# Chunk totals from a float32 exp row by POOL transfers, half of the score masks on ScalarE and GpSimd, and late first outputs, in a gated linear attention and squared-ReLU MLP kernel

## The chip, the cores and the metric

The kernel runs on one core of a Trainium2 chip. The metric is the device time in microseconds (us) of one launch. The engines are TensorE (PE, with PEld for its weight loads), VectorE (DVE), ScalarE (ACT), GpSimd (POOL) and SyncE (SP, which here issues loads and stores).

## The reference

For 4 batches and 8 heads, 768 time steps of a gated recurrence on a 48 x 48 state, then an MLP over all 3072 tokens:

```python
for t in range(S):                                   # S = 768
    state = alpha[:, :, t, :, None] * state + einsum('bhd,bhe->bhde', k[:, :, t], v[:, :, t])
    y[:, :, t] = einsum('bhd,bhde->bhe', q[:, :, t], state)
x = y.transpose(0, 2, 1, 3).reshape(B * S, H * D)    # 3072 x 384
h = x @ w_in                                         # 384 -> 2048
r = maximum(h, 0.0)
out = (r * r) @ w_out                                # 2048 -> 384
```

All inputs and the output are float32; the kernel's matmuls run in bfloat16.

## The kernel before, in words

The 3072 tokens are 24 chunks (tiles) of 128 tokens, six for each batch. Chunks 0 to 3 are done as two sets of two chunks with a layout of their own (`add_set`), chunks 4 to 23 one by one (`add_chunk`).

One chunk goes through these steps. ACT takes the logarithm of alpha into `L_s` (L600). PE multiplies it by a triangular matrix (`e_p0`, L610), which gives running sums down the chunk in a PSUM bank, and with four more matmuls of one column against a vector of ones (L612) the sum over the whole chunk, laid out with the state's rows on the partitions. ACT writes exp of the running sums as `A` (L619) and of their negatives as `Ainv` (L623), both bfloat16, and exp of the totals into `ae_s` by two small activations (L626, L629). DVE multiplies q by `A` into `qA_s` (L638) and k by `Ainv` into `kI_s` (L641). PE transposes both, DVE copies them to `qkT`. PE forms the scores in two banks a chunk (`add_scores`); from chunk 8 on two chunks' scores are one step that needs four banks. DVE multiplies each half of the scores by the triangular mask (`e_sm`, L675, 512 columns, twice a chunk). PE adds k times v onto the state (`e_ps`), DVE scales the state by the totals in `ae_s` (`e_stm`, L696), ACT casts it to `sb` (L701); the next chunk's state step and its output matmuls (`e_p3a`) need `sb`. PE forms the outputs (`e_p3a`, `e_p3b`), ACT casts them to `xn`, PE transposes them, and DVE copies them to `xT_big` (`e_xT`), which the MLP reads. POOL casts v to `vb` (L605) and the MLP's weights (L330).

The MLP works on groups of tiles, `GN = [4, 1, 1, 2, 2, ...]`. `add_moe1` is the first matmul, with a relu on ACT (L798) and a square on DVE (L811) into `gT`. The second is `add_moe2`, or, for groups 3 to 10, `add_moe2_pair`, which computes two tiles with seven half-size products in place of eight. That needs sums of blocks of `gT` (S1 to S4): S1 and S2 are DVE additions into buffers of the pool `stage` (L928), S3 and S4 are, where the group is in `BY_DMA`, accumulating transfers issued by POOL (L936). Outputs go out through SP (L853, L855, L1021).

The order of every engine's instructions is written out when the kernel is built. A planner (`Plan`) holds each step as an `Op` with an assumed duration, its dependencies, a priority (lower is earlier) and the banks that it takes, and picks step by step what can start first; the steps are then emitted in order of their planned starts, and each engine runs its own in that order. A chunk's `e_p0` may not be planned before `s <= LEAD + progress`, where progress counts the MoE work planned so far in tiles of 5.12 us. `OUT_LATE0` and `OUT_LATE` delay the store of an output by so many planned microseconds (group 0: 16, others: 3.5). `DMA_FROM`, `BUSY` and `XT_ACT` choose from which group the accumulating transfers are used and from which chunk some copies go to ACT. PE runs filler matmuls only ahead of the first second-layer matmul.

Times in the diff, such as 0.6 or 3.6, are the planner's assumptions.

Of the kernel before, what the change touches and what calls it, by code (L numbers as in the profile page):

```python
# [8 lines left out]
FP32 = mybir.dt.float32  # L9
# [55 lines left out]
class Plan:  # L65


    def __init__(self):
        self.pending = {}
        self.order = []  # L70
        self.free = {}
        self.pool = []
        self.outs = []

    def add(self, op):
        op.durs = op.eng if isinstance(op.eng, dict) else {op.eng: op.dur}
        for e in op.durs:
            self.pending.setdefault(e, []).append(op)
        return op

    def ready(self, op):
        t = op.at
        slack = PE_SLACK if "PE" in op.durs else 0.0
        if slack and self.free.get("PE", 0.0) > PE_CALM:
            slack = 0.25
        for d, x in op.deps:
            if d.done is None:
                return None
            if x is None:
                t = max(t, d.done + (slack if d.eng != "PE" else 0.0))  # L90
            else:
                t = max(t, d.start + d.dur + x)
        if op.takes is not None:
            free = [(sl.free_at(), i) for i, sl in enumerate(op.takes)]
            free = sorted((f, i) for f, i in free if f is not None)[:op.n_slots]
            if len(free) < op.n_slots:
                return None
            op.slots = [op.takes[i] for _, i in free]
            op.slot = op.slots[0]
            t = max(t, free[-1][0])  # L100
        return t
# [59 lines left out]
def kernel(  # L161
# [10 lines left out]
    nc = tc.nc  # L172
# [77 lines left out]
    NBUF = 4  # L250
    DMA_FROM = 0
    BY_DMA = {g: ("S3", "S4") if g >= DMA_FROM else () for g in range(40)}
    BUSY = 99
    CP_N = 99
    XT_ACT = 0
    L_s = big.tile([P, NBUF, H, DP], BF16)
# [4 lines left out]
    nc.vector.memset(kI_s[:, :, :, D:], 0.0)  # L261
    ae_s = big.tile([P, NBUF, NP, 2], FP32)
    nc.vector.memset(ae_s, 0.0)
# [9 lines left out]
    def pin(ins):  # L273
        tc.keep_in_program_order(ins)
# [96 lines left out]
    def add_set(u):  # L371
# [24 lines left out]
        def add_decay(a):  # L396
# [14 lines left out]
            def e_exp(out, nm, scale):  # L411
                out[a] = work.tile([P, 2, HH, D], BF16, name=nm)
                pin(nc.scalar.activation(out[a], pm[a][:, 0:HD].rearrange("p (j h d) -> p j h d", j=2, h=HH), AF.Exp, scale=scale))
# [19 lines left out]
        def e_ae(h):  # L433
            r = slice(64 * h, 64 * h + 64)
            pin(nc.scalar.activation(ae[r, :, :, h].rearrange("q c p -> q p c"),
                                     pm[0][r, HD:HD + 2 * NP].rearrange("q (p c) -> q p c", c=2), AF.Exp))
# [63 lines left out]
        def add_state(c):  # L500
# [18 lines left out]
            def e_stm():  # L519
                st4 = e["st"].rearrange("p n (j e) -> p n j e", j=2)  # L520
                pin(nc.vector.tensor_mul(st4, st4, bcast(ae[:, c], D)))
            stm = add("DVE", 0.47, e_stm, ps, ae1, **gs)
# [6 lines left out]
        def add_out(c):  # L529
# [28 lines left out]
            def e_xn():  # L558
                e["xn"] = work.tile([P, HD], BF16, name="xn")
                cast2(xn, e["xn"], e["py"][:, 0:HD])  # L560
# [21 lines left out]
    def add_chunk(s):  # L582
# [25 lines left out]
        def e_p0():  # L608
            pm = d["pm"] = psum(p0, [P, 512], FP32)
            mm(pm[:, 0:HD], lhsT=utri_b[:, 0, :], rhs=L[:, :, 0:D], start=True, stop=True)  # L610
            for p in range(NP):
                mm(pm[:, HD + p:HD + p + 1], lhsT=L[:, 2 * p:2 * p + 2, :], rhs=ones_col,  # L612
                   start=True, stop=True)
        p0 = Op("PE", 0.27, e_p0, [ln], takes=GLA_BANKS, lat=0.05, **g)
        p0.gla = s

        def e_A():
            d["A"] = work.tile([P, H, D], BF16, name="A")
            pin(nc.scalar.activation(d["A"], d["pm"][:, 0:HD].rearrange("p (h d) -> p h d", h=H), AF.Exp))  # L619

        def e_Ai():
            d["Ai"] = work.tile([P, H, D], BF16, name="Ainv")
# [10 lines left out]
        ae0 = add("ACT", 0.18, e_ae0, p0, after(ai), **g)  # L633
        ae1 = add("ACT", 0.19, e_ae1, p0, after(ae0), **g)
        p0.gives = ae1

        def e_qA():
            pin(nc.vector.tensor_mul(qA[:, :, 0:D], d["qt"], d["A"]))  # L638

# [30 lines left out]
        p2, first = d["p2"]  # L670

        def e_sm(hh):
            if hh == 0:
                d["sm"] = work.tile([P, 2, NP, P], BF16, name="sm")
            pin(nc.vector.tensor_mul(d["sm"][:, hh], d["sc"][hh], utri_b.to_broadcast([P, NP, P])))  # L675
        done = after(p2, -0.15) if first else p2
        sm0 = add("DVE", 0.6, lambda: e_sm(0), done, **g)
        sm1 = add("DVE", 0.6, lambda: e_sm(1), done, after(sm0), **g)
        p2.gives += [sm0, sm1]

        if not last:
# [8 lines left out]
            if c == 0 and s:  # L690
                prev = C[s - 2]["sb"]
            ps = plan.add(Op("PE", 0.17, e_ps, [mk, vb, ae1, prev], lat=0.16, **g))

            def e_stm():
                st4 = d["st"].rearrange("p n (j e) -> p n j e", j=2)
                pin(nc.vector.tensor_mul(st4, st4, bcast(ae, D)))  # L696
            stm = add("DVE", 0.47, e_stm, ps, ae1, prio=-2.0)

# [20 lines left out]
        if c > 0:  # L719
            p3a = plan.add(Op("PE", 0.17, e_p3a, [cp, C[s - 1]["sb"], after(sm0)], takes=GLA_BANKS, **g))  # L720
        p3b = plan.add(Op("PE", 0.25, e_p3b, [after(sm1, 0.02), sm0, vb, after(p3a)], takes=None if c else GLA_BANKS, lat=0.15, **g))

        def e_xn():
            d["xn"] = work.tile([P, HD], BF16, name="xn")
            cast(xn, d["xn"], d["py"][:, 0:HD])
# [15 lines left out]
    def add_scores(ss):  # L741
# [24 lines left out]
    OUT_LATE = 3.5  # L766
    OUT_LATE0 = 16
    RELU_PRIO = -20.0
# [6 lines left out]
    def add_moe1(g, f0, before, lo=0, hi=None, per=1):  # L775
# [27 lines left out]
        def e_sq():  # L803
# [7 lines left out]
            pin(nc.vector.tensor_mul(dst, r, r))  # L811
        fr = sq[(g - NGT, "free")] if g >= NGT else None
        o = add("DVE", 0.06 + w / 1850.0, e_sq, rl, fr, prio=SQ_PRIO)
        o.shared = True
# [5 lines left out]
    def add_moe2(g, tt, before, box, quarters, pools):  # L820

        for qd in quarters:
# [17 lines left out]
        def e_ev():  # L840
            box["ob"] = opool.tile([P, d_model], FP32, name="ob")
# [7 lines left out]
        def e_out():  # L849
# [191 lines left out]
    for g in range(NG):  # L1041
# [9 lines left out]
        if g == 0:  # L1051
            boxes = [dict() for _ in range(GN[0])]
            for part in FIRST_PARTS:
                for tt in range(GN[0]):
                    b2 = add_moe2(0, tt, b2, boxes[tt], part, FIRST)
        else:
            pools = M2_LAST if g >= NG - 2 else M2_BANKS
            if g in PAIR_SUMS or (g in (1, 2) and JOIN):
# [6 lines left out]
                if g == 2:  # L1065
                    sq[(1, "free")] = b2
# [70 lines left out]
```

## Time and profile before

| | |
|---|---|
| time, median of 3 runs | 184.35 us (184.28 to 184.57) |
| the profiled execution | 184.13 us, of which 182.4 us are its span |
| TensorE clock granted | 1.000 |
| PE busy | 175.6 us (96%) |
| DVE busy | 150.3 us (82%) |
| ACT busy | 122.4 us (67%) |
| POOL busy | 41.7 us (23%) |
| HBM | 25.17 MB read, 4.72 MB written |

The span runs from the first to the last instruction; the rest of the time lies around it. Busy times are unions of the instructions' intervals on an engine. A group's line gives line, engine, operation, output<-inputs, shapes, count | busy us, mean ns of one | idle time before it, and what ended that. A matmul's interval includes its way through the pipeline, so matmuls that follow each other overlap.

### The profile page before, as it was taken

To read this page: it belongs to the slowest core of one execution; us is meant where nothing else is said; L and a number is where in the kernel's file an instruction comes from. 1 tells how busy PE (TensorE), PEld (TensorE's weight loads), DVE (VectorE), ACT (ScalarE), POOL (GpSimd) and SP (SyncE) were. 2 spreads that over 40 slices of the span, in tenths; PEclk is the share of its full clock that TensorE was granted. 3 is DMA by queue.
4 is the path that set the end of the run, shared out by engine and by line. 5 is a ranking of instruction groups with operands and counts; after the bars stand their busy time and mean duration, and the time that the engine had idled before them with its cause. 6 is when DMAs were issued, how large, how long until landed. Compare 5 with 4: busy or idle time off the path is not lost.

```text
span 182.4 us, 5636 instructions
## 1 busy us (share of the span) xinstructions
PE 175.6 (96%) x2248; PEld 147.9 (81%) x2248; DVE 150.3 (82%) x330; ACT 122.4 (67%) x295; POOL 41.7 (23%) x59
## 2 busy tenths in 40 slices
PE   7998999999999999999999999999999999999992
PEld 2676788667776887899899899899898899899871
DVE  6599869749989699999998999899998997865310
ACT  3576579436868688976867779666778777657321
POOL 4013575251111101504024002125005004030000
PEclk9999999999999999999999999999999999999999
DMA  5999998899999779999999989999999705316113
GB/s 143 264 264 340 380 351 165 278 232 172 195 194 168 155 185 202 193 198 186 229 191 205 242 190 178 215 225 212 252 174 204 184 4 101 104 33 128 43 55 117
DMA packets 101529, 34.43 MB, mean 189 GB/s; under 512 B 92416, under 2 KB 98304, under 8 KB 101504
## 3 DMA queue, kind: packets, MB, share of 16 engines
q1 hardware_dynamic: 99200, 29.89, 75.2%
q0 software_dynamic: 2304, 4.20, 13.2%
q8 instruction: 17, 0.28, 0.7%
q14 instruction: 8, 0.07, 0.1%
HBM read 25.17 MB, written 4.72 MB: 164 GB/s over the span
## 4 chain that ended last, share of the span: by engine, by line
PE 68%; DVE 16%; SPq 5%; DMA 4%; ACT 2%; issue 2%; POOL 0%; ACTq 0%
PE bank L277 61%; PE bank L280 6%; SPq L366 5%; DVE sm L675 4%; DMA wi<-in_moe_w_in_dram 4%; DVE gT L811 2%; DVE foldT L896 2%; DVE qkT L595 2%; PE st L277 1%; DVE kI_s L641 1%; DVE sums L928 1%; DVE st L696 1%; ACT r L798 1%; DVE xT_big L595 1%; DVE ob L985 1%
## 5 line engine op out<-in xcount | busy, mean ns | idle before, releaser
L277 PE MATMUL bank<-xT_big,w_in_b 128*128 128x256 bf16 (+1 forms) x624 | 76.1, 264 | 0.9 <-POOL w_in_b L330 0.7
L798 ACT ACTIVATE r<-bank 128x512 bf16<-128x512 f32 x96 | 56.8, 600 | 18.3 <-PE bank L277 14.8
L277 PEld LDWEIGHTS <-w_in_b 128*128 128x128 bf16 x624 | 53.4, 98 | 6.8 <-POOL w_in_b L330 0.8
L811 DVE TENSOR_TENSOR gT<-r 128x512 bf16<-128x512 bf16 x96 | 42.8, 469 | 8.7 <-ACT r L798 8.4
L277 PE MATMUL bank<-w_out_b,gT 128*128 128x192 bf16 (+1 forms) x320 | 44.1, 278 | 0.1
L277 PEld LDWEIGHTS <-gT 128*128 128x128 bf16 x448 | 37.9, 98 | 6.8 <-DMA gT<-sums 0.3
L605 POOL CAST vb<-vt_s 128x384 bf16<-128x384 f32 x20 | 13.4, 691 | 53.1 <-DMA vt_s<-in_v_dram 48.6
L675 DVE TENSOR_TENSOR sm<-bank,utri_b 128x512 bf16<-128x512 f32 x40 | 24.9, 681 | 0.5 <-PE bank L277 0.5
L936 POOL DMA_DIRECT2D gT<-gT x8 | 6.9, 861 | 42.9 <-DVE sums L928 34.2
L595 DVE COPY qkT<-bank 128x1024 bf16<-128x1024 bf16 x20 | 13.7, 683 | 1.1 <-PE bank L280 1.0
L638 DVE TENSOR_TENSOR qA_s<-qt_s,A 128x384 bf16<-128x384 f32 x20 | 12.4, 620 | 2.1 <-ACT A L619 1.9
L619 ACT ACTIVATE A<-bank 128x384 bf16<-128x384 f32 x20 | 9.9, 496 | 5.5 <-PE bank L277 5.5
L277 PE MATMUL bank<-foldT,sums 128*128 128x192 bf16 x128 | 13.2, 246 | 0.0
L277 PE MATMUL bank<-foldT,gT 128*128 128x192 bf16 x128 | 13.2, 246 | 0.0
L277 PEld LDWEIGHTS <-qkT 64*128 64x128 bf16 (+1 forms) x228 | 9.1, 95 | 3.6 <-issue 1.9
L641 DVE TENSOR_TENSOR kI_s<-kt_s,Ainv 128x384 bf16<-128x384 f32 x20 | 11.9, 595 | 0.0
L600 ACT ACTIVATE L_s<-at_s 128x384 bf16<-128x384 f32 x20 | 10.5, 524 | 1.0 <-DMA at_s<-in_alpha_dram 0.7
L277 PEld LDWEIGHTS <-sums 128*128 128x128 bf16 x128 | 10.7, 98 | 0.4
L701 ACT CAST sb<-st 128x384 bf16<-128x384 f32 x16 | 7.6, 476 | 4.9 <-DVE st L696 4.8
L593 ACT CAST xn<-bank 128x384 bf16<-128x384 f32 x20 | 9.7, 484 | 1.8 <-PE bank L277 1.6
L277 PE MATMUL bank<-vb,sm 128*128 128x48 bf16 (+1 forms) x224 | 10.2, 183 | 0.1
L280 PE MATMUL bank<-ident_bf,qA_s 128*128 128x128 bf16 x96 | 9.3, 220 | 0.6 <-DVE qA_s L419 0.4
(93 smaller groups left out, 234.9 us busy)
## 6 DMA issues: line engine op xcount, KB each, us to landing
at_s<-in_alpha_dram SPq DMA_DIRECT2D x22, 192.0 KB, 5.0
qt_s<-in_q_dram SPq DMA_DIRECT2D x22, 192.0 KB, 4.9
kt_s<-in_k_dram SPq DMA_DIRECT2D x22, 192.0 KB, 4.5
vt_s<-in_v_dram SPq DMA_DIRECT2D x20, 192.0 KB, 4.8
out_dram<-ob SPq DMA_DIRECT2D x20, 192.0 KB, 3.5
wo<-in_moe_w_out_dram SPq DMA_DIRECT2D x4, 768.0 KB, 6.7
wi<-in_moe_w_in_dram SPq DMA_DIRECT2D x3, 768.0 KB, 7.8
gT<-gT POOLq DMA_DIRECT2D x8, 256.0 KB, 4.8
```

The costliest lines, as they stand in the source:

```text
L277: pin(nc.tensor.matmul(*a, **kw))
L280: pin(nc.tensor.transpose(*a))
L593: pin(nc.scalar.copy(out_t, in_t))
L595: pin(nc.vector.tensor_copy(out_t, in_t))
L600: pin(nc.scalar.activation(L[:, :, 0:D], d["at"], AF.Ln))
L605: pin(nc.gpsimd.tensor_copy(d["vb"], d["vt"]))
L619: pin(nc.scalar.activation(d["A"], d["pm"][:, 0:HD].rearrange("p (h d) -> p h d", h=H), AF.Exp))
L638: pin(nc.vector.tensor_mul(qA[:, :, 0:D], d["qt"], d["A"]))
L641: pin(nc.vector.tensor_mul(kI[:, :, 0:D], d["kt"], d["Ai"]))
L675: pin(nc.vector.tensor_mul(d["sm"][:, hh], d["sc"][hh], utri_b.to_broadcast([P, NP, P])))
L798: pin(nc.scalar.activation(box["r"][:, 0:w], box["ph"][:, 0:w], AF.Relu))
L811: pin(nc.vector.tensor_mul(dst, r, r))
```

## The change

What is changed, in the order of the diff:

- `Plan.held` and `wide`: a step of lower priority may not take a bank that the four-bank scores step could use, while that step waits for nothing but banks.
- `DMA_FROM = 6`: S3 and S4 of groups 3, 4 and 5 are DVE additions; groups 6 to 10 keep the accumulating transfers.
- `BUSY = 8`, `XT_ACT = 1`: from chunk 8 on the copy into `xT_big` is on ACT.
- The totals of chunks 4 to 23: the four one-column matmuls and the two small exps are gone. `A` is written in float32, with its inner order changed, so that its last row (partition 127) holds each half of the totals as one run; two transfers issued by POOL bring that row to `ae_s`, whose layout is changed to fit. `A` of the sets is float32 too; the sets keep their matmuls for the totals.
- From chunk 8 on the second half of the scores is copied by ACT, unmasked, to SBUF, and GpSimd zeroes what the mask would (`affine_select`). The first half stays a product on DVE.
- `A`, `Ainv` and `xn` have three buffers instead of four.
- Outputs: group 0's four tiles are kept in one buffer of `stage` and stored 32 planned microseconds after they are ready; groups 1 and 2 (chunks 4 and 5) 12 after; the others 3.5 as before. The sums of the pairs wait for the pair three back, instead of four, to be done with its buffer.
- `S_PRIO = -12`: sums go ahead of the chunks' steps on DVE. `LEAD = 5`.
- Second-layer matmuls of group 0 wait for the squares of their own two tiles only.

The diff, cut to that:

```diff
+    def held(self, op):
+        for w in self.wide:
+            if w is not op and w.start is None and w.prio < op.prio and all(d.done is not None for d, _ in w.deps):
+                return w.takes
+        return ()
...
-            free = [(sl.free_at(), i) for i, sl in enumerate(op.takes)]
+            held = self.held(op)
+            free = [(sl.free_at(), i) for i, sl in enumerate(op.takes) if sl not in held]
...
-    DMA_FROM = 0
+    DMA_FROM = 6
-    BUSY = 99
+    BUSY = 8
-    XT_ACT = 0
+    XT_ACT = 1
...
-    ae_s = big.tile([P, NBUF, NP, 2], FP32)
+    ae_s = big.tile([P, NBUF, 2, NP], FP32)
...
+    SEL_FROM, SEL_T, SEL_N = 8, 0.6, 1
+    RESERVE = 1
+    ROW_POOL, ROW_LAT, ROW_DMA = 0.95, 3.6, 0.15
...
-            for p in range(NP):
-                mm(pm[:, HD + p:HD + p + 1], lhsT=L[:, 2 * p:2 * p + 2, :], rhs=ones_col,
-                   start=True, stop=True)
-        p0 = Op("PE", 0.27, e_p0, [ln], takes=GLA_BANKS, lat=0.05, **g)
+        p0 = Op("PE", 0.165, e_p0, [ln], takes=GLA_BANKS, lat=0.10, **g)
...
-            d["A"] = work.tile([P, H, D], BF16, name="A")
-            pin(nc.scalar.activation(d["A"], d["pm"][:, 0:HD].rearrange("p (h d) -> p h d", h=H), AF.Exp))
+            d["A32"] = work.tile([P, 2, D, NP], FP32, name="A", bufs=3)
+            d["A"] = d["A32"].rearrange("q j d p -> q p j d")
+            pin(nc.scalar.activation(d["A"], d["pm"][:, 0:HD].rearrange("q (p j d) -> q p j d", p=NP, j=2), AF.Exp))
...
-        def e_ae0():
-            pin(nc.scalar.activation(ae[0:64, :, 0], d["pm"][0:64, HD:HD + NP], AF.Exp))
-
-        def e_ae1():
-            pin(nc.scalar.activation(ae[64:128, :, 1], d["pm"][64:128, HD:HD + NP], AF.Exp))
+        def e_ae(h):
+            pin(nc.gpsimd.dma_start(out=ae[64 * h:64 * h + D, h, :], in_=d["A32"][P - 1:P, h]))
...
+        aes = [add("POOL", ROW_POOL, lambda h=h: e_ae(h), a_, old, lat=ROW_LAT, **g) for h in range(2)]
...
+        def e_sc():
+            pin(nc.scalar.copy(sm_half(1), d["sc"][1]))
+
+        def e_sel():
+            pin(nc.gpsimd.affine_select(out=sm_half(1), in_=sm_half(1), compare_op=ALU.is_ge, fill=0.0,
+                                        base=0, pattern=[[0, NP], [1, P]], channel_multiplier=-1))
...
+        if s >= SEL_FROM and s % SEL_N == 0:
+            sm0 = add("DVE", 0.6, lambda: e_sm(0), done, **g)
+            sc1 = add("ACT", 0.485, e_sc, done, **g)
+            sm1 = add("POOL", SEL_T, e_sel, sc1, prio=-20.0)
+            p2.gives += [sm0, sc1]
...
-            ps = plan.add(Op("PE", 0.17, e_ps, [mk, vb, ae1, prev], lat=0.16, **g))
+            ps = plan.add(Op("PE", 0.17, e_ps, [mk, vb, prev], lat=0.16, **g))
...
-            stm = add("DVE", 0.47, e_stm, ps, ae1, prio=-2.0)
+            stm = add("DVE", 0.47, e_stm, ps, *aes, prio=-2.0)
...
-    OUT_LATE0 = 16
+    OUT_LATE0 = 32
+    OUT_LATE1 = 12
+    KEEP0 = 1
...
-            deps = [o for f in fs for o in sq[(g, f)]] + ...
+            deps = [o for f in fs for o in sq_of(g, tt, f)] + ...
...
+            if g == 0 and KEEP0:
+                if "ob" not in state:
+                    state["ob"] = stage.tile([P, GN[0], d_model], FP32, name="ob0", tag="stage")
+                box["ob"] = state["ob"][:, tt]
...
-        add("OUT", 0.65, e_out, ev, at=0.0).late = OUT_LATE if g else OUT_LATE0
+        add("OUT", 0.65, e_out, ev, at=0.0).late = OUT_LATE if g > 2 else OUT_LATE1 if g else OUT_LATE0
...
-        used = pairs_done[-4] if len(pairs_done) > 3 else []
+        used = pairs_done[-3] if len(pairs_done) > 2 else []
...
-    S_PRIO = -1
+    S_PRIO = -12
...
-    LEAD = 4
+    LEAD = 5
```

More of the change, by code (lines that the diff above doesn't have):

```diff
@@ L73, in __init__ @@
         self.outs = []
+        self.wide = []
     def add(self, op):
@@ L288 @@
     PAIRED = 7
+    SEL_FROM, SEL_T, SEL_N = 8, 0.6, 1
+    RESERVE = 1
+    ROW_POOL, ROW_LAT, ROW_DMA = 0.95, 3.6, 0.15
     JOIN = 0
+    PAIRS0 = 0
+    ORDERED = 1
+    PAIR0_BANKS = FIRST0 = sl_bank[4:0:-1]
+    ORDER0 = ["i", "i", "i", "i", "i", "o", "o", 4, "o", "o", 5]
     SET_BANKS = [sl_bank[0:4] + sl_bank[5:7], sl_bank[0:3] + sl_bank[5:7]]
@@ L411, in e_exp @@
             def e_exp(out, nm, scale):
-                out[a] = work.tile([P, 2, HH, D], BF16, name=nm)
+                out[a] = work.tile([P, 2, HH, D], FP32 if nm == "A" else BF16, name=nm, bufs=3)
                 pin(nc.scalar.activation(out[a], pm[a][:, 0:HD].rearrange("p (j h d) -> p j h d", j=2, h=HH), AF.Exp, scale=scale))
@@ L434, in e_ae @@
             r = slice(64 * h, 64 * h + 64)
-            pin(nc.scalar.activation(ae[r, :, :, h].rearrange("q c p -> q p c"),
+            pin(nc.scalar.activation(ae[r, :, h, :].rearrange("q c p -> q p c"),
                                      pm[0][r, HD:HD + 2 * NP].rearrange("q (p c) -> q p c", c=2), AF.Exp))
@@ L520, in e_stm @@
                 st4 = e["st"].rearrange("p n (j e) -> p n j e", j=2)
-                pin(nc.vector.tensor_mul(st4, st4, bcast(ae[:, c], D)))
+                pin(nc.vector.tensor_mul(st4, st4, bcast(ae[:, c].rearrange("q j p -> q p j"), D)))
             stm = add("DVE", 0.47, e_stm, ps, ae1, **gs)
@@ L558, in e_xn @@
             def e_xn():
-                e["xn"] = work.tile([P, HD], BF16, name="xn")
+                e["xn"] = work.tile([P, HD], BF16, name="xn", bufs=3)
                 cast2(xn, e["xn"], e["py"][:, 0:HD])
@@ L610, in e_p0 @@
             mm(pm[:, 0:HD], lhsT=utri_b[:, 0, :], rhs=L[:, :, 0:D], start=True, stop=True)
-            for p in range(NP):
-                mm(pm[:, HD + p:HD + p + 1], lhsT=L[:, 2 * p:2 * p + 2, :], rhs=ones_col,
-                   start=True, stop=True)
-        p0 = Op("PE", 0.27, e_p0, [ln], takes=GLA_BANKS, lat=0.05, **g)
+        p0 = Op("PE", 0.165, e_p0, [ln], takes=GLA_BANKS, lat=0.10, **g)
         p0.gla = s
         def e_A():
-            d["A"] = work.tile([P, H, D], BF16, name="A")
-            pin(nc.scalar.activation(d["A"], d["pm"][:, 0:HD].rearrange("p (h d) -> p h d", h=H), AF.Exp))
+            d["A32"] = work.tile([P, 2, D, NP], FP32, name="A", bufs=3)
+            d["A"] = d["A32"].rearrange("q j d p -> q p j d")
+            pin(nc.scalar.activation(d["A"], d["pm"][:, 0:HD].rearrange("q (p j d) -> q p j d", p=NP, j=2), AF.Exp))
         def e_Ai():
-            d["Ai"] = work.tile([P, H, D], BF16, name="Ainv")
+            d["Ai"] = work.tile([P, H, D], BF16, name="Ainv", bufs=3)
             pin(nc.scalar.activation(d["Ai"], d["pm"][:, 0:HD].rearrange("p (h d) -> p h d", h=H), AF.Exp, scale=-1.0))
-        def e_ae0():
-            pin(nc.scalar.activation(ae[0:64, :, 0], d["pm"][0:64, HD:HD + NP], AF.Exp))
-        def e_ae1():
-            pin(nc.scalar.activation(ae[64:128, :, 1], d["pm"][64:128, HD:HD + NP], AF.Exp))
+        def e_ae(h):
+            pin(nc.gpsimd.dma_start(out=ae[64 * h:64 * h + D, h, :], in_=d["A32"][P - 1:P, h]))
         plan.add(p0)
@@ L632, in add_chunk @@
         ai = add("ACT", 0.38, e_Ai, p0, after(a_), **g)
-        ae0 = add("ACT", 0.18, e_ae0, p0, after(ai), **g)
-        ae1 = add("ACT", 0.19, e_ae1, p0, after(ae0), **g)
-        p0.gives = ae1
+        p0.gives = ai
+        aes = [add("POOL", ROW_POOL, lambda h=h: e_ae(h), a_, old, lat=ROW_LAT, **g) for h in range(2)]
+        for x in aes:
+            x.quiet, x.moves = True, ROW_DMA
         def e_qA():
-            pin(nc.vector.tensor_mul(qA[:, :, 0:D], d["qt"], d["A"]))
+            pin(nc.vector.tensor_mul(qA[:, :, 0:D].rearrange("q (p j) d -> q p j d", j=2),
+                                     d["qt"].rearrange("q (p j) d -> q p j d", j=2), d["A"]))
         def e_kI():
@@ L670, in add_chunk, with sm_half @@
         p2, first = d["p2"]
+        def sm_half(hh):
+            if "sm" not in d:
+                d["sm"] = work.tile([P, 2, NP, P], BF16, name="sm")
+            return d["sm"][:, hh]
         def e_sm(hh):
-            if hh == 0:
-                d["sm"] = work.tile([P, 2, NP, P], BF16, name="sm")
-            pin(nc.vector.tensor_mul(d["sm"][:, hh], d["sc"][hh], utri_b.to_broadcast([P, NP, P])))
-        done = after(p2, -0.15) if first else p2
-        sm0 = add("DVE", 0.6, lambda: e_sm(0), done, **g)
-        sm1 = add("DVE", 0.6, lambda: e_sm(1), done, after(sm0), **g)
-        p2.gives += [sm0, sm1]
+            pin(nc.vector.tensor_mul(sm_half(hh), d["sc"][hh], utri_b.to_broadcast([P, NP, P])))
+        def e_sc():
[3 more added lines that the diff above has]
+                                        base=0, pattern=[[0, NP], [1, P]], channel_multiplier=-1))
+        done = after(p2, -0.15) if first else p2
+        if s >= SEL_FROM and s % SEL_N == 0:
[3 more added lines that the diff above has]
+            p2.gives += [sm0, sc1]
+        else:
+            sm0 = add("DVE", 0.6, lambda: e_sm(0), done, **g)
+            sm1 = add("DVE", 0.6, lambda: e_sm(1), done, after(sm0), **g)
+            p2.gives += [sm0, sm1]
         if not last:
@@ L691, in add_chunk @@
                 prev = C[s - 2]["sb"]
-            ps = plan.add(Op("PE", 0.17, e_ps, [mk, vb, ae1, prev], lat=0.16, **g))
+            ps = plan.add(Op("PE", 0.17, e_ps, [mk, vb, prev], lat=0.16, **g))
             def e_stm():
                 st4 = d["st"].rearrange("p n (j e) -> p n j e", j=2)
-                pin(nc.vector.tensor_mul(st4, st4, bcast(ae, D)))
-            stm = add("DVE", 0.47, e_stm, ps, ae1, prio=-2.0)
+                pin(nc.vector.tensor_mul(st4, st4, bcast(ae.rearrange("q j p -> q p j"), D)))
+            stm = add("DVE", 0.47, e_stm, ps, *aes, prio=-2.0)
             def e_sb():
@@ L720, in add_chunk @@
             p3a = plan.add(Op("PE", 0.17, e_p3a, [cp, C[s - 1]["sb"], after(sm0)], takes=GLA_BANKS, **g))
-        p3b = plan.add(Op("PE", 0.25, e_p3b, [after(sm1, 0.02), sm0, vb, after(p3a)], takes=None if c else GLA_BANKS, lat=0.15, **g))
+        p3b = plan.add(Op("PE", 0.25, e_p3b, [after(sm1, 0.02 if sm1.eng == "DVE" else 0.15), sm0, vb, after(p3a)], takes=None if c else GLA_BANKS, lat=0.15, **g))
         def e_xn():
-            d["xn"] = work.tile([P, HD], BF16, name="xn")
+            d["xn"] = work.tile([P, HD], BF16, name="xn", bufs=3)
             cast(xn, d["xn"], d["py"][:, 0:HD])
@@ L753, in add_scores @@
         plan.add(p2)
+        if len(ss) > 1 and RESERVE:
+            plan.wide.append(p2)
         for s in ss:
@@ L811, in e_sq @@
             pin(nc.vector.tensor_mul(dst, r, r))
-        fr = sq[(g - NGT, "free")] if g >= NGT else None
-        o = add("DVE", 0.06 + w / 1850.0, e_sq, rl, fr, prio=SQ_PRIO)
+        fr = sq[(g - NGT, "free")] if g >= NGT else []
+        o = add("DVE", 0.06 + w / 1850.0, e_sq, rl, *fr, prio=SQ_PRIO)
         o.shared = True
@@ L829, in add_moe2 @@
             fs = range(qd * FT // NQ, (qd + 1) * FT // NQ) if g == 0 else range(FT)
-            deps = [o for f in fs for o in sq[(g, f)]] + [w_dep("o", fs[-1] if g == 0 else FT - 1)] + ([after(before)] if before else [])
+            deps = [o for f in fs for o in sq_of(g, tt, f)] + [w_dep("o", fs[-1] if g == 0 else FT - 1)] + ([after(before)] if before else [])
             op = plan.add(Op("PE", 0.65, e_mm, deps, takes=pools if qd == 0 else None, prio=0.1 + 0.01 * g))
@@ L840, in e_ev @@
         def e_ev():
-            box["ob"] = opool.tile([P, d_model], FP32, name="ob")
+            if g == 0 and KEEP0:
+                if "ob" not in state:
+                    state["ob"] = stage.tile([P, GN[0], d_model], FP32, name="ob0", tag="stage")
+                box["ob"] = state["ob"][:, tt]
+            else:
+                box["ob"] = opool.tile([P, d_model], FP32, name="ob")
             if ev.eng == "DVE":
@@ L861 @@
     parts = []
-    DMA_ORDER = A0 + B0 + Z0 + A1 + Z1 + ["i", "i", "i", "i", "i", "o", "o", 4, "o", "o", 5]
+    DMA_ORDER = A0 + B0 + Z0 + A1 + Z1 + ORDER0
     for d in DMA_ORDER + list(range(6, NT)):
@@ L1053 @@
             for part in FIRST_PARTS:
-                for tt in range(GN[0]):
+                for tt in range(GN[0] - 2 * PAIRS0):
                     b2 = add_moe2(0, tt, b2, boxes[tt], part, FIRST)
+            ends = [b2]
+            if PAIRS0:
+                T = add_fold()
+            for i in range(GN[0] - 2 * PAIRS0, GN[0], 2):
+                ends.append(add_moe2_pair([(0, i), (0, i + 1)], b2 if ORDERED else None, T, PAIR0_BANKS))
+            sq[(0, "free")] = ends
         else:
@@ L1065 @@
                 if g == 2:
-                    sq[(1, "free")] = b2
+                    sq[(1, "free")] = [b2]
             else:
@@ L1071 @@
                     b2 = add_moe2(g, tt, b2, {}, range(NQ), pools)
-        sq[(g, "free")] = b2
-    LEAD = 4
+        if g:
+            sq[(g, "free")] = [b2]
+    LEAD = 5
     def gate(op):
```

## The prediction

> **What bounds the kernel now.** I read the page's first two parts, then the table by stage, the groups by line and form, the timeline around one chunk, and the answers for single tiles and lines.
>
> ```profile
> span 182.4 us, 5636 instructions
> ...
> PE 175.6 (96%) x2248; PEld 147.9 (81%) x2248; DVE 150.3 (82%) x330; ACT 122.4 (67%) x295; POOL 41.7 (23%) x59
> ...
> PEclk9999999999999999999999999999999999999999
> DMA  5999998899999779999999989999999705316113
> ```
>
> ```profile
> 40.00:60.00 20.00, 19.54 (x266) 14.77 (x264) 18.41 (x35) 14.26 (x37) 2.58 (x4) 1.00 1.13 183
> 60.00:100.00 40.00, 39.94 (x535) 35.37 (x533) 37.67 (x82) 31.41 (x80) 9.29 (x13) 1.00 1.04 193
> 100.00:150.00 50.00, 49.90 (x686) 45.45 (x684) 47.95 (x106) 36.74 (x93) 9.09 (x13) 1.00 0.95 191
> ```
>
> Columns of the second fence: stage, its length, then PE, PEld, DVE, ACT, POOL busy, clock, DMA share, GB/s. The clock is full throughout, so PE time is work plus waiting. PE is filled from the first MoE matmul at 18.4 us to the last at 179.2: 39.94 of 40 us and 49.90 of 50. The page stretches a matmul by its pipeline, so I also took distances between starts in the timeline, where a 256-column matmul follows the last after 0.109 us. By those, some 1.3 us of waiting lies in 45 to 55 us (before turned q and k and the scores, one relu), and under 1 us in all the rest. DVE, at 94 to 96% from 60 to 150 us, is the second limit; DMA is as full until 142 us. So time falls when PE work goes, and rises when an engine that was at its edge makes PE's fixed order wait.
>
> **The totals' matmuls.** Each of the 20 chunks loses four one-column matmuls.
>
> ```profile
> 46.64 0.34 PE L277 MATMUL bank<-L_s,utri_b 128*128 128x384 bf16 x1
> ...
> 46.82 0.24 PE L277 MATMUL bank<-ones_t,L_s 128*128 128x1 bf16 x4
> ...
> 46.92 1.00 PE L277 MATMUL bank<-xT_big,w_in_b 128*128 128x128 bf16 x15
> ```
>
> They hold PE from 46.82 to the next start at 46.92: 0.10 us a chunk, not the 0.24 shown. 20 x 0.10 = 2.0 us, on the path because PE never rests there. The two small exps go too (L626 and L629, 3.5 + 3.4 us on ACT).
>
> **The row transfers.** In their place come 40 issues on POOL, each moving one row of 192 floats to 48 partitions as 48 pieces of 16 bytes. Nearest rows, POOL's accumulating transfers:
>
> ```profile
> L936 POOL DMA_DIRECT2D gT<-gT x8: 841/843/993, 73.1 to 162.0; - x8
> ...
> DMA to landing us min/median/max: 3.3/5.0/7.3
> ```
>
> Issue: 40 x 0.86 = 34 us of POOL, between 0 and 40 us; POOL is idle for 140. Landing: the rows moved 256 KB under load, this moves 768 bytes; bounds 0 and 7.3, and I take 3.3, the lower end, since data is little. [...]
>
> The chain from the start of A to the next chunk's state matmul becomes: A 0.5, two issues 1.8, landing 3.3, state multiply 0.56, cast to sb 0.48, hand-overs 0.3: 6.9 us. In the trace A starts 7.0 us (chunk 8: 57.1 to 64.1) to 15 us before that matmul; most chunks have 8.4 to 10.5 (chunk 12: 79.7 to 88.1; chunk 15: 98.5 to 108.5). So it is hidden, barely in 45 to 65 us, and LEAD 5 lets each A go one chunk earlier, about 5 us of MoE work. Cost 0 by the cover; without it, what it exceeds times the hand-over, for at most 16 hand-overs. The state multiply would wait at the head of DVE's order, with squares queued behind it, and PE behind those. I put +0.3 us, range 0 to +4.
>
> The transfers' share of the DMA engines: 40 x 48 = 1920 pieces. A piece costs 22 ns by the loads' queue (75.2% of 16 x 182.4 us over 99200) and 167 ns by POOL's (13.2% over 2304): 2.6 to 20 us over 16 engines. I take the low end, nearer in size. The six accumulating transfers dropped for groups 3 to 5 give back 6 x 1.5 = 9 us.
>
> **The float32 A.** Exp to 384 floats: ACT's float32 copy of the same shape takes 481 ns against 496 for A now, so 0. The product with q reads both inputs as float32, A in steps of 16 bytes; the state multiply, float32 throughout, takes 555 ns, the q product with nothing beside it 547 to 559. I take 0. No row shows this step; at worst a doubling, 20 x 0.4 = 8 us of DVE, inside what follows; no gain, as the width of q stays.
>
> **Engines traded.** Chunks 8 to 23 lose a mask (0.68) and the copy to xT_big (0.35) on DVE: 16 x 1.03 = 16.5 us. Groups 3 to 5 add back six sums at 0.69: 4.1. ACT gains a 512-column copy (0.60, the relu's row) and the 384-column copy (0.48): 16 x 1.08 = 17.3, less 6.9 of the small exps: +10.4. POOL gains 16 selects: 64 columns took 244 ns, 128 took 289, so 512 about 0.56 us (an estimate from these; a cast of 384 took up to 0.83). What POOL does beside DVE is not free:
>
> ```profile
> 42.66 0.73 POOL L605 CAST vb<-vt_s 128x384 bf16<-128x384 f32 x1 [2.74 <-DMA vt_s<-in_v_dram]
> ...
> 42.94 0.86 DVE L641 TENSOR_TENSOR kI_s<-kt_s,Ainv 128x384 bf16<-128x384 f32 x1
> ```
>
> The k product takes 0.55 alone and 0.86 beside the cast. Squares met by a cast average 0.70 against 0.42; masks stay at 0.68 with or without, POOL's issues slow nothing. At 0.28 a meeting, 16 selects cost DVE 4.5 us, at most 16 x 0.56 = 9. [...] DVE still comes out lighter: -16.5 + 4.1 + 4.5 = -7.9.
>
> For 100 to 150 us, eight chunks: DVE 47.95 - 8.2 + 2.2 = 42 of 50 us; ACT 36.74 + 8 x 0.73 = 42.6. Neither is full. Half-masks now end by copy and select, 0.60 + 0.56, instead of two masks in series, 1.3; the price is POOL's queue, where a select may stand behind an issue (0.86) or a cast, with the output matmuls (p3b) waiting and all PE behind them. The order puts selects first and other matmuls between; 0, in the +0.3 above. From 60 to 75 us DVE is not yet relieved, and the added sums go ahead of the chunks' work: 2 x 0.69 a pair, covered because the masks of chunk 8 on leave in the same stretch.
>
> **The late outputs.** Group 0's eight issues and chunk 4's sit in front of loads on SP:
>
> ```profile
> 56.81 0.99 SPq L352 DMA_DIRECT2D at_s<-in_alpha_dram  x1
> 57.89 4.88 SPq L853 DMA_DIRECT2D out_dram<-ob  x6
> 62.88 0.51 SPq L352 DMA_DIRECT2D qt_s<-in_q_dram  x1
> ```
>
> The load of q for that chunk starts about 5 us later than it could. With 32 and 12 us of delay these ten issues pass some 16 loads, into 74 to 92 us, where DMA has the 9 us that the dropped transfers leave, and where loads wait for their buffers as well (SP waits 3.5 us for k products and 3.3 for squares between 20 and 100 us). They then hold up loads needed a chunk or more ahead. Together with one more chunk of lead I credit 0.5 of the 1.3 us of waiting in 45 to 55 us, range 0 to 1.3. One buffer of stage goes to these outputs; the sums of each pair keep three and use them in turn. Reserving banks for the double scores, finer waits for group 0's squares, three buffers for A, Ainv and xn, and the new layout of ae_s change order, not work: 0.
>
> **Sum.** The profiled execution: 184.13 us, of it 182.42 span and 1.71 around it; start (18.4) and tail (3.2 after PE's last) stay. 184.13 - 2.0 - 0.5 + 0.3 = 181.93. The median of the runs is 0.22 higher, so the forecast for the median is 182.1 us.
>
> **Rivals.** *Late totals (slower).* POOL's single queue would carry 34 us of issues, 9 of selects, 13 of casts and 9 of transfers, and rows would queue behind a transfer or a cast that waits for its load (POOL waits 48.6 us for v now, up to 9.4 at a time). It decides where landing plus queueing exceeds 3.4 us at the tight hand-overs and about 5 at the rest, since 6.9 - 3.3 = 3.6 is fixed. With 5.0, the median row, plus one 0.86 issue ahead, the chain is 9.5: over by up to 2.5 where 7.0 to 8.6 are available, say 8 of 16 hand-overs by 0.5 on average after LEAD: +4 in place of +0.3, so 185.8. For it: the DMA row is full until 142 us. Against: one chunk more of lead, lighter DMA. Chance 0.24.
>
> *Nothing gained.* The freed 2.0 us on PE is eaten by relus that wait behind ACT's extra copies and squares that wait for selects: 182.1 + 2.1 = 184.2. It would need ACT near 95%; I have 85% in 100 to 150. To this belongs the change not doing what it says, a new order in which PE waits where the matmuls were. Chance 0.08.
>
> *More gained.* All of the 1.3 us, and another 0.7 of the small waits after 60 us, where DVE ends the wait: 182.1 - 0.8 - 0.3 - 0.7 = 180.3. Chance 0.08.
>
> **Numbers.** Forecast 0.60, its own range 180.9 to 183.4. Faster by over 0.2% (about what a measurement of this kernel can tell; 0.37 us): 0.60 + 0.08 = 0.68. Within: 0.06 of nothing gained. Slower: 0.24 + 0.02 = 0.26. The range runs from 180.3, the larger gain, to 185.4, which takes in nothing gained and the cheaper half of late totals.
>
> **What would show it.** PE's matmuls fall by 80 and its busy time by about 2 us; DVE near 142, ACT near 133, POOL near 85 us. Right: the state multiply shows hardly any wait for a DMA into ae_s, and PE starts have no gaps near state matmuls. Wrong: DVE idle before L696 by that DMA, landings over 5 us, row issues far behind A on POOL; or ACT over 90% in 100 to 150 us with PE waiting for relus; or a first MoE matmul or tail that moved by over 0.5 us.

## The result, and the profile after

The changed kernel takes 190.81 us (median of 4 runs, 190.57 to 191.04) against 184.46 us for the kernel before on the same chip: 1.033 times the time, with an interval of 1.028 to 1.038. It is 6.4 us slower, where 2.3 us less was forecast. Times are medians of all executions, and ratios use only those outside a slower state of the chip, so a ratio can differ a little from the quotient of two medians. The profiled execution took 190.57 us, 188.8 of it span. Its page, first the lines that answer to those shown of before:

```profile
span 188.8 us, 5557 instructions
...
PE 177.1 (94%) x2168; PEld 146.0 (77%) x2168; DVE 149.4 (79%) x303; ACT 135.2 (72%) x288; POOL 68.0 (36%) x109
```

The table by stage of the changed kernel (stage, length, PE, PEld, DVE, ACT, POOL busy, clock, DMA share, GB/s):

```profile
40.00:60.00 20.00, 18.01 (x233) 13.45 (x232) 18.57 (x32) 13.22 (x28) 5.23 (x10) 1.00 1.11 180
60.00:100.00 40.00, 37.77 (x473) 31.68 (x472) 36.65 (x71) 35.02 (x77) 15.46 (x27) 1.00 1.04 182
100.00:150.00 50.00, 49.28 (x619) 43.85 (x617) 45.94 (x92) 42.47 (x92) 21.73 (x35) 1.00 0.86 157
```

The 80 matmuls are gone (2168 instead of 2248). But PE now rests: 1.99 us from 40 to 60, 2.23 from 60 to 100 and 0.72 from 100 to 150, where before it rested 0.46, 0.06 and 0.10. The groups by line and form name what grew (mean ns of one after the comma); first the two lines of before, then those of the changed kernel:

```profile
L619 ACT ACTIVATE A<-bank 128x384 bf16<-128x384 f32 x20 | 9.9, 496 | 5.5 <-PE bank L277 5.5
L638 DVE TENSOR_TENSOR qA_s<-qt_s,A 128x384 bf16<-128x384 f32 x20 | 12.4, 620 | 2.1 <-ACT A L619 1.9
...
L632 ACT ACTIVATE A<-bank 128x384 f32<-128x384 f32 x20 | 17.7, 883 | 2.2 <-PE bank L285 2.1
L649 DVE TENSOR_TENSOR qA_s<-qt_s,A 128x384 bf16<-128x384 f32 x20 | 17.1, 857 | 4.5 <-ACT A L632 4.2
```

A took 496 ns before and takes 883; the q product took 620 on average (548 median) and takes 857. Both lie between PE's running sums (`e_p0`) and PE's transposes, and PE's order is fixed. The timeline shows at one chunk how that reaches PE:

```profile
48.09 0.87 ACT L632 ACTIVATE A<-bank 128x384 f32<-128x384 f32 x1 [0.49 <-PE bank L285]
48.75 0.53 ACT L636 ACTIVATE Ainv<-bank 128x384 bf16<-128x384 f32 x1
48.99 0.84 DVE L649 TENSOR_TENSOR qA_s<-qt_s,A 128x384 bf16<-128x384 f32 x1 [0.22 <-ACT A L632]
49.75 0.55 DVE L653 TENSOR_TENSOR kI_s<-kt_s,Ainv 128x384 bf16<-128x384 f32 x1
49.89 0.40 PE L288 MATMUL bank<-ident_bf,qA_s 128*128 128x128 bf16 x4 [0.62 <-DVE qA_s L649]
```

The bracket is the idle time of the engine just before: PE stood for 0.62 us until the q product was there. The k product, 0.55 us here as before, starts 0.76 us after the q product (median of the twenty 0.78) where it used to start 0.47 us after. Over all chunks PE's weight loads waited 3.5 us for q products and 3.3 us for k products, against 1.1 and 0.2 before. The planner reckons with 0.38 us for A and 0.47 for the product.

The row transfers did what they should. Their answer in the trace:

```profile
L639 POOL DMA_DIRECT2D ae_s<-A x40: 504/504/688, 33.9 to 156.9; - x40
...
  DVE st L724: 1.5, 1
...
DMA to landing us min/median/max: 1.6/3.6/5.2
```

The middle line is who waited for a row to land: the state multiply, once, 1.5 us.

### The profile page after: what moved, and what is told of

It is laid out like the page before. It is cut to its first block, busy times and chain, and to the rows that moved or that the text cites. A ratio compares the mean times of both kernels' runs of the same rounds, so it can differ in the third digit from the quotient of the medians.

```text
span 188.8 us, 5557 instructions
## 1 busy us (share of the span) xinstructions
PE 177.1 (94%) x2168; PEld 146.0 (77%) x2168; DVE 149.4 (79%) x303; ACT 135.2 (72%) x288; POOL 68.0 (36%) x109
## 4 chain that ended last, share of the span: by engine, by line
PE 65%; ACT 9%; DVE 9%; issue 6%; SPq 5%; DMA 3%; POOL 0%; ACTq 0%; DVEq 0%
PE bank L285 58%; PE bank L288 6%; SPq L381 5%; DMA wi<-in_moe_w_in_dram 3%; DVE kI_s L653 3%; ACT A L632 3%; ACT r L830 2%; ACT Ainv L636 2%; PE st L285 1%; DVE gT L843 1%; ACT xn L608 1%; DVE foldT L933 1%; DVE gT L975 1%; DVE qkT L610 1%; DVE sums L965 1%
## 5 line engine op out<-in xcount | busy, mean ns | idle before, releaser
L285 PE MATMUL bank<-xT_big,w_in_b 128*128 128x256 bf16 (+1 forms) x624 | 74.3, 264 | 1.6 <-DVE xT_big L610 1.0
L285 PEld LDWEIGHTS <-w_in_b 128*128 128x128 bf16 x624 | 54.9, 98 | 8.7 <-issue 1.5
L843 DVE TENSOR_TENSOR gT<-r 128x512 bf16<-128x512 bf16 x96 | 44.8, 489 | 7.1 <-ACT r L830 6.9
L639 POOL DMA_DIRECT2D ae_s<-A x40 | 20.6, 521 | 46.2 <-ACT A L632 43.1
L649 DVE TENSOR_TENSOR qA_s<-qt_s,A 128x384 bf16<-128x384 f32 x20 | 17.1, 857 | 4.5 <-ACT A L632 4.2
L632 ACT ACTIVATE A<-bank 128x384 f32<-128x384 f32 x20 | 17.7, 883 | 2.2 <-PE bank L285 2.1
L696 POOL TENSOR_SCALAR_AFFINE_SELECT sm<-sm 128x512 bf16<-128x512 bf16 x16 | 10.5, 676 | 20.6 <-ACT sm L693 20.6
L690 DVE TENSOR_TENSOR sm<-bank,utri_b 128x512 bf16<-128x512 f32 x24 | 15.4, 684 | 3.0 <-PE bank L285 3.0
L288 PE MATMUL bank<-ident_bf,kI_s 128*128 128x128 bf16 x96 | 9.4, 220 | 1.8 <-DVE kI_s L653 1.5
L636 ACT ACTIVATE Ainv<-bank 128x384 bf16<-128x384 f32 x20 | 10.8, 540 | 0.0
```

The lines of the kernel that those rows point to most:

```text
L285: pin(nc.tensor.matmul(*a, **kw))
L288: pin(nc.tensor.transpose(*a))
L639: pin(nc.gpsimd.dma_start(out=ae[64 * h:64 * h + D, h, :], in_=d["A32"][P - 1:P, h]))
L649: pin(nc.vector.tensor_mul(qA[:, :, 0:D].rearrange("q (p j) d -> q p j d", j=2), d["qt"].rearrange("q (p j) d -> q p j d", j=2), d["A"]))
L690: pin(nc.vector.tensor_mul(sm_half(hh), d["sc"][hh], utri_b.to_broadcast([P, NP, P])))
```

## The experiments

All ratios are to the kernel before, run on the same chip. In the changed layout of A the exp and the q product go through their elements in an order in which neighbours lie four floats, 16 bytes, apart: that is the step. Theory 1: this step is slow on both engines. Theory 2: the copies and selects overload ScalarE and POOL. Theory 3: the new order is worse. In e1, e6, e7 and e9 values of A or of the totals are permuted, and e10 leaves the totals out; the instructions and their shapes stay, but for the rows in e10.

**e1_plain_a.** One part undone.

```diff
-            d["A"] = d["A32"].rearrange("q j d p -> q p j d")
+            d["A"] = d["A32"].rearrange("q j d p -> q (j d p)").rearrange("q (p j d) -> q p j d", p=NP, j=2)
```

> The changed kernel with one thing undone: A is written and read in the plain order, so that neither ScalarE nor VectorE steps by 16 bytes; still float32, the row transfers still move 768 bytes, but the totals that they bring are in another order than the state's rows (that part of the result is not the reference's). The order of the instructions on every engine is the changed kernel's. Theory 1 (the step of 16 bytes makes A and the q product slow, and PE waits behind them): A about 0.49 us and the q product about 0.55 us, as before; PE's waits fall from about 13 us to 6 or 7, and the time to 183 to 185 us. Theory 2 (ScalarE's copies and GpSimd's selects overload the chain) and theory 3 (the new order itself is worse): 189 us or more, as the step has little to do with it.

184.94 us; 1.0016 (0.9985 to 1.0047). The groups:

```profile
L649 DVE TENSOR_TENSOR qA_s<-qt_s,A 128x384 bf16<-128x384 f32 x20 | 11.6, 581 | 1.9 <-ACT A L632 1.8
...
L632 ACT ACTIVATE A<-bank 128x384 f32<-128x384 f32 x20 | 10.0, 501 | 2.3 <-PE bank L285 2.1
```

Still float32, same order of instructions, same transfers, and the whole loss is gone. Float32 as such costs nothing (501 ns against 496 in bfloat16). Theories 2 and 3 fall as causes of the loss. The forecast gain is not there either; that is taken up at e9.

**e2_stride_before.** The suspect alone, in the kernel before (three buffers for A, Ainv and xn to make room).

```diff
-            d["A"] = work.tile([P, H, D], BF16, name="A")
...
+            d["A32"] = work.tile([P, 2, D, NP], FP32, name="A", bufs=3)
+            d["A"] = d["A32"].rearrange("q j d p -> q p j d")
...
```

> The kernel before with one thing added: A in float32, written and read in steps of 16 bytes as in the changed kernel (A, Ainv and xn with three buffers to make room). The totals' matmuls, masks, outputs and the plan stay. Theory 1: A about 0.88 and the q product about 0.86 us, 188 to 191 us. Theories 2 and 3: at most 1 us above the kernel before, 184.5 to 185.5 us, since ScalarE has room (67% busy).

193.20 us; 1.0445 (1.0380 to 1.0511). The step alone costs more than the whole change, and more than theory 1 gave it. That DVE was fuller there (94 to 96% from 60 to 150 us in the kernel before) may be why; it is not shown.

**e3_no_select.** `SEL_FROM = 99`.

> The changed kernel with both halves of the masks on VectorE again (no ScalarE copy, no select). Theory 1: not better, 190 to 193 us, as VectorE gets 16 x 0.68 us back and A stays slow. Theory 2: much better, 186 us or less. Theory 3: 189 to 191 us.

194.23 us; 1.0506 (1.0460 to 1.0552), just above what theory 1 gave. Against the changed kernel, with A as slow, the half-masks on ScalarE and GpSimd save 3 us; they are no part of the loss.

**e5_old_totals.** The changed kernel with the matmuls, the small exps and the bfloat16 A of before.

```diff
+            for p in range(NP):
+                mm(pm[:, HD + p:HD + p + 1], lhsT=L[:, 2 * p:2 * p + 2, :], rhs=ones_col, start=True, stop=True)
...
-        aes = [add("POOL", ROW_POOL, lambda h=h: e_ae(h), a_, old, lat=ROW_LAT, **g) for h in range(2)]
+        aes = [ae1]
```

> The changed kernel with the totals as before: four one-column matmuls and two small exps for each chunk, A in bfloat16 and plain order, no row transfers; selects, late outputs, order and lead as changed. Theory 1: 183.5 to 186 us. Theories 2 and 3: 189 us or more (theory 2 more than now, as ScalarE gets the small exps back).

184.53 us; 0.9994 (0.9956 to 1.0031). Everything but the totals (selects, copies on ScalarE, late outputs, lead, reserved banks) is worth nothing measurable, although DVE's busy time falls from 150.3 to 141.2 us:

```profile
PE 175.0 (96%) x2248; PEld 148.1 (81%) x2248; DVE 141.2 (77%) x304; ACT 133.7 (73%) x327; POOL 46.5 (25%) x69
```

PE was full before and is full here; relieving DVE alone gives PE nothing to do sooner.

**e6_write_only and e7_read_only.** The two sides of the step, each alone, in the changed kernel's order: in e6 the q product reads the plain view of e1, in e7 the exp writes through it.

> The changed kernel, in its order, with A written by ScalarE in steps of 16 bytes but read by the q product in plain order (so q is multiplied by a permuted A: that part of the result is not the reference's). If both sides of the step cost: A 0.88, the q product 0.55 to 0.60, and about half of the changed kernel's loss, 187 to 189 us. If ScalarE's write alone matters: 190 us; if VectorE's read alone matters: 184.5 to 185.5 us, as with the plain A.

> The counterpart: A written plain, read by the q product in steps of 16 bytes (the values are permuted, as in the run before it). If both sides cost: A 0.50, the q product 0.86, 187 to 189 us. If ScalarE's write alone matters: 184.5 to 185.5 us; if VectorE's read alone matters: 190 us.

e6: 187.87 us, 1.0179 (1.0153 to 1.0206), A 883 ns, the product 557. e7: 188.85 us, 1.0213 (1.0174 to 1.0253), A 500, the product 891. Both sides cost, about equally. Over e1 they add 1.6% and 2.0%, together 3.6%, against 3.1% for the changed kernel over e1: nearly a plain sum.

**e4_true_plan.** The planner, which had 0.38 us for A and 0.47 for the product, is told 0.77 us for each: 0.39 and 0.30 more, about the measured growth.

> The changed kernel with the planner told what A and the q product take (0.77 us each in place of 0.38 and 0.47), so that the order leaves room for them; nothing else differs. The cause is the step of 16 bytes either way; this asks how it costs time. Theory 1a (PE waits because the order was made for a shorter chain): the waits mostly go, 184 to 187 us. Theory 1b (the longer chain or the load on ScalarE and VectorE costs time in any order): 188.5 us or more.

191.68 us; 1.0347 (1.0301 to 1.0393). Theory 1a falls: the order that this planner makes for the longer durations does not hide them. Its windows:

```profile
40.00:60.00 20.00, 18.14 (x221) 13.80 (x220) 17.77 (x32) 12.48 (x25) 5.09 (x9) 0.91 1.15 183
60.00:100.00 40.00, 39.45 (x476) 33.85 (x475) 38.57 (x76) 34.35 (x74) 16.89 (x26) 1.00 1.03 190
100.00:150.00 50.00, 47.80 (x629) 42.76 (x627) 44.55 (x91) 40.76 (x87) 22.96 (x38) 1.00 0.85 161
```

PE's rests mostly move: 1.86, 0.55 and 2.20 us, where the changed kernel had 1.99, 2.23 and 0.72. The granted clock was 0.91 in the first stage and 0.987 over the span; this execution took 191.94 us, one at a clock of 1.000 took 190.63.

**e8_row_apart.** A in bfloat16 and plain; a third exp on partitions 96 to 127 writes the row's order for the transfers, into a single buffer.

```diff
+        def e_row():
+            d["A32"] = work.tile([P, 2, D, NP], FP32, name="row", bufs=1)
+            pin(nc.scalar.activation(d["A32"].rearrange("q j d p -> q p j d")[P - 32:P],
+                                     d["pm"][P - 32:P, 0:HD].rearrange("q (p j d) -> q p j d", p=NP, j=2), AF.Exp))
...
```

> A version that gives the reference's result without the step on the way to q: A in bfloat16 and plain order as before, and after Ainv a third exp on the last 32 partitions alone, in float32 and in the row's order, which the row transfers read (one buffer; the planner is told 0.77 us for it and 0.5 for a transfer's issue). Everything else as changed. If only the chain to q and k matters: A 0.49, the q product 0.55, 183 to 185.5 us, though ScalarE works about 13 us more than with the plain A. If ScalarE's load matters: 186 us or more.

192.45 us; 1.0426 (1.0374 to 1.0479). A miss for the cheap repair.

```profile
L635 ACT ACTIVATE row<-bank 32x384 f32<-32x384 f32 x20 | 17.3, 866 | 2.3 <-DMA ae_s<-row 1.9
```

On 32 partitions the stepped write takes as long as on 128, and now it is 17.3 us of extra work. The chain that ended last runs through ScalarE for 17% of the span, for 1% in e1. What exactly carries the work to PE stays open: squares waited 14.9 us for relus (6.9 in the changed kernel), the state multiply 3.1 us for late rows, and the row's exp, as the line shows, 1.9 us for transfers out of its one buffer, with ScalarE's other work behind it; these were not separated. ScalarE's load alone does not explain it: from 60 to 150 us it is busy for 79.8 us here and 81.2 us in e5, and PE rests 5.7 us here and 0.2 us in e5.

**e11_inner_p and e12_bf16_step.** Where the step must lie to be slow. In e11 both instructions run through their elements in A's own order, so that the step moves to the PSUM read, to q and to qA_s. In e12, the kernel before has A in bfloat16 in the changed order, in steps of 8 bytes (one run).

> The changed kernel, with the reference's result, but A's exp and the q product run through their elements in the order in which A lies in SBUF: A is then written and read without a step, and the steps (384 bytes in float32) fall on the PSUM read of ScalarE and on q and qA_s. If only a step on A's side of SBUF is slow: A 0.50, the q product 0.55 to 0.6, and 184.5 to 185.5 us as with the plain A. If a step on any operand is as slow: 0.88 and 0.86 or more, 190 us or more. Mixed: one of them slow, 187 to 189.

> The kernel before with A kept in bfloat16 but written and read in the changed kernel's order, that is in steps of 8 bytes (A, Ainv and xn with three buffers). If the time follows the distance in bytes, or float32: A and the q product clearly under 0.88 and 0.86. If it follows the step in elements: as in float32.

e11 took 206.46 us (two of its four executions 204.72 and 204.85), 1.111 (1.106 to 1.116); e12 191.22 us. The groups of e11, then of e12:

```profile
L649 DVE TENSOR_TENSOR qA_s<-qt_s,A 128x384 bf16<-128x384 f32 x20 | 37.9, 1895 | 1.8 <-ACT A L632 1.8
...
L632 ACT ACTIVATE A<-bank 128x384 f32<-128x384 f32 x20 | 9.9, 498 | 2.6 <-PE bank L285 2.4
```

```profile
L620 ACT ACTIVATE A<-bank 128x384 bf16<-128x384 f32 x20 | 20.8, 1039 | 4.4 <-PE bank L277 4.3
...
L639 DVE TENSOR_TENSOR qA_s<-qt_s,A 128x384 bf16<-128x384 f32 x20 | 13.2, 658 | 7.9 <-ACT A L620 7.9
```

ScalarE pays for a stepped write to SBUF (883 ns in float32, 1039 in bfloat16), not for a PSUM read in steps of 384 bytes (498). VectorE pays for steps of 16 bytes in its float32 input (857) and far more with q and qA_s stepped (1895), but a bfloat16 A in steps of 8 bytes costs it nothing (median 559, against 548 in plain order). Expected were a result that follows bytes or one that follows elements; the two engines differ.

**e9_rows_after_v and e10_no_rows.** Where the 2.0 us of the matmuls went. In e1 PE stood at three places where it had not before, 1.0 us at 49.8, 1.0 at 70.6 and 0.5 at 104.6 us, and before each a cast of v ran beside DVE products that took longer than alone (two squares in 1.38 us for 2 x 0.42, k products in 0.74 and 0.93 for 0.55). At the second:

```profile
70.16 0.62 ACT L636 ACTIVATE Ainv<-bank 128x384 bf16<-128x384 f32 x1
...
70.44 0.69 POOL L620 CAST vb<-vt_s 128x384 bf16<-128x384 f32 x1
70.81 0.74 DVE L653 TENSOR_TENSOR kI_s<-kt_s,Ainv 128x384 bf16<-128x384 f32 x1
71.61 0.40 PE L288 MATMUL bank<-ident_bf,kI_s 128*128 128x128 bf16 x4 [0.83 <-DVE kI_s L653]
```

The product takes 0.74 us beside the cast where it takes 0.55 alone, so the cast explains 0.2 of the 1.0 us there; the product could start only at 70.81, when Ainv was there. The cast stands behind row issues on POOL (before, 13 of the 20 ran as soon as v had landed). e9 makes the row transfers depend on `vb`; e10 leaves them out.

> The plain A (totals permuted, as in the first run of that name), and in the plan each chunk's two row transfers wait for the cast of its v, so that on POOL the cast is issued first, as it was in the kernel before; the planner makes a new order from that. With the plain A the 2.0 us of the totals' matmuls came back as new PE waits beside squares and k products that a late cast of v held up. If those late casts are the cause: PE's waits fall by 1 to 2.5 us, 182.5 to 184 us. If not: 184.5 us or more.

> The plain A, in that order, with the row transfers left out altogether (the totals stay zero, so the state's part of the result is not the reference's). If the row transfers (their time on POOL, the casts behind them, late totals) turned the saved 2.0 us into waits: 182 to 183.2 us. If the waits come from the selects, ScalarE's copies or the order: 184.3 us or more.

e9: 184.23 us, 0.9991 (0.9963 to 1.0018): between the two readings (up to 184, or 184.5 and more), so it doesn't decide. e10: 183.56 us, 0.9944 (0.9908 to 0.9981). Against e1 the rows thus cost 0.7%, some 1.3 us, by two runs whose intervals just miss each other. Even with none the gain is 1.0 us, not 2.0. Of what is missing 0.4 us lies behind PE: in the profiles of e1, e5, e10, e14 and the changed kernel the span ends 4.1 us after PE's last matmul starts, in those of before, e9 and e16 3.7 us after; why is not shown.

**e14, e15, e16.** What e11 and e12 point to: A in bfloat16 in the row's order, written in that order by ScalarE (step on the PSUM read) and read by VectorE in steps of 8 bytes. e15 adds e9's dependency, e16 also tells the planner 0.5 us for a row's issue instead of 0.95.

```diff
-            d["A32"] = work.tile([P, 2, D, NP], FP32, name="A", bufs=3)
+            d["A32"] = work.tile([P, 2, D, NP], BF16, name="A", bufs=3)
...
-            pin(nc.scalar.activation(d["A"], d["pm"][:, 0:HD].rearrange("q (p j d) -> q p j d", p=NP, j=2), AF.Exp))
+            pin(nc.scalar.activation(d["A32"], d["pm"][:, 0:HD].rearrange("q (p j d) -> q j d p", p=NP, j=2), AF.Exp))
...
-    ae_s = big.tile([P, NBUF, 2, NP], FP32)
+    ae_s = big.tile([P, NBUF, 2, NP], BF16)
```

> The changed kernel, in its order, with A and ae_s in bfloat16 and A's exp run in the order in which A lies (ScalarE then writes without a step and steps in its PSUM read, 0.50 us in the run with the inner p; VectorE reads A in steps of 8 bytes, 0.56 to 0.66 us in the one look at bfloat16). The totals are valid, rounded to bfloat16. If the slow steps are the whole loss: A 0.50, the q product 0.56 to 0.62, 184 to 185.5 us. If float32's size or the transfers matter beside the steps: 186.5 us or more.

> The same, with each chunk's row transfers planned behind the cast of its v. If late casts held up VectorE: 0.3 to 1.2 us below the run before it, 183.3 to 184.5 us. If not: the same or slower.

> The same again, with the planner told 0.5 us for a row transfer's issue, as measured, in place of 0.95. If the order on POOL still cost something: 183 to 184 us, below the kernel before. If the 2.0 us is spent on waits of other kinds: 184 us or more.

e14: 185.05 us, 0.9994 (0.9967 to 1.0021), the changed kernel's order to the instruction, with

```profile
L649 DVE TENSOR_TENSOR qA_s<-qt_s,A 128x384 bf16<-128x384 f32 x20 | 11.6, 582 | 1.7 <-ACT A L632 1.6
L632 ACT ACTIVATE A<-bank 128x384 bf16<-128x384 f32 x20 | 10.0, 499 | 2.0 <-PE bank L285 1.9
```

So the slow steps are the whole loss, with valid totals too. e15: 184.60 us, 0.9976 (0.9950 to 1.0003), just above the range for late casts and not clear of e14, so it doesn't decide either. e16: 183.86 us, 0.9940 (0.9911 to 0.9968), which beats both kernels: 0.6% under the kernel before, with totals rounded to bfloat16. The cast of v is ahead of the rows there and POOL's plan is true; which of the two gives how much is not separated, as each makes a new order.

## Why the prediction was wrong, step by step

**What bounds the kernel**: right. PE was full, and time rose with PE's waits. PE's last matmul starts at 184.7 us instead of 178.8, 5.9 us later; with 2.0 us less work that is 7.9 us more waiting. The other 0.5 us of the 6.4 lies behind it.

**The float32 A: the step that failed.** The prediction put "so 0" for the exp and "I take 0" for the product. The exp's price came from a float32 copy that writes its elements side by side; width was matched, the step was not. Measured: 0.39 us more, 7.7 us of ScalarE. For the product the bound of 0.4 us a chunk was the author's estimate, which no row gave; for this step it held (measured 0.31 over the median), but it was set against DVE's freed busy time ("inside what follows"). What it cost was not busy time: the product lies on the path from `e_p0` to the transposes, in series with the exp, and e6, e7 and e1 show each side worth some 3 to 4 us. The right entry was up to 20 x 0.7 = 14 us on a path that PE waits for, of which 5.9 (the changed kernel less e1) came through, and no rival had it.

**The totals' matmuls**: 2.0 us left PE as forecast, but did not become time. The best that the runs show of it is about 1 us (0.6% in e10 and e16); the rest is explained only in part.

**The row transfers**: issue was put at 0.86 us and took 0.52, landing at 3.3 and took 3.6; hidden, as forecast, with one wait of 1.5 us. What was not forecast is that they cost some 1.3 us elsewhere (e10 against e1). That they do it by pushing the casts of v back into DVE's products fits the traces but was not settled (e9, e15), though the prediction had priced such meetings at 0.28 us.

**Engines traded**: ScalarE forecast 133, measured 135.2 (129.5 without the steps, e14); DVE 142 against 149.4 (144.9 in e14); POOL 85 against 68. A select took 0.63 us (median) for the 0.56 estimated. Seven squares met a select and no cast; they averaged 0.59 us against 0.42 for those that met nothing, 0.17 a meeting for the 0.28 taken. The table was about right and did not matter, since e5 shows that DVE's relief is worth nothing here.

**The late outputs**: credited with 0.5 us. In e5, which has them, nothing shows in the time. Group 0's eight issues, at 57.9 to 65.2 us before, stand at 71.2 to 75.6, less late than the 74 to 92 told; five of them:

```profile
71.16 3.10 SPq L890 DMA_DIRECT2D out_dram<-ob  x5
```

**Rivals**: *late totals* had the right sign and the wrong mechanism; its mark, DVE idle before the state multiply, is 1.5 us in all. *Nothing gained* and *more gained* did not happen either. The time of the first, 184.2 us, is near what the kernel takes once the step is removed (e1, e14), but its mechanism was not what failed: ScalarE was at 85% from 100 to 150 us, as forecast. Of the signs listed for a wrong forecast only landings over 5 us showed, barely (5.2 at most); none of them looked at A's own duration.

What stays open: why a step costs each engine what it does, why an order made for the true durations (e4) does not hide them, how e8's extra exp reaches PE, and where the rest of the 2.0 us of the matmuls goes.

## What to carry to other kernels

When an operand changes its layout, look for a row with the same step, not only the same type and size, and if there is none, price the instruction at twice its time on the path that it lies on, whatever its engine's busy share (here a stepped A, where it cost anything, cost 1.6 to 2.1 times, stepped q and output 3.4 times). A layout that suits a transfer may be had by letting the producer run in the output's order and step on its PSUM side, as e14 does (0.50 us for A). Here the first engine was full, and removing work from the second gained nothing (e5); work removed from the first showed only in part (e10, e16).

## What the runs showed of the hardware

A 384-column exp by ScalarE took 0.50 us with side-by-side writes in float32 or bfloat16, 0.88 in float32 steps of 16 bytes, 1.04 in bfloat16 steps of 8, and 0.50 again with the step on the PSUM read; in the 16-byte steps 32 partitions took 0.87 (e8), as long as 128. A VectorE product of 384 columns took 0.55 us, 0.86 with one float32 input in steps of 16 bytes, and 1.87 (median) with q and the output stepped. A 768-byte row to 48 partitions took POOL 0.50 us to issue against 0.84 for a 256 KB transfer, and landed 1.6 to 5.2 us later, with a DMA share of 0.86 to 1.11 in the three stages from 40 to 150 us.
